# Where the second pair of heads gets its rotated keys and queries: GpSimd and DMAs in place of TensorE

## The chip, the cores and the metric

The kernel runs on one core of a Trainium2 chip. A core has TensorE (PE; its weight loads are listed as PEld), VectorE (DVE), ScalarE (ACT), GpSimd (POOL), a sync engine (SP) whose queue issues most DMAs, and 16 DMA engines. Each engine runs its own instructions in their written order and waits on semaphores. The metric is the device time in microseconds (us) of one execution, as a median of runs.

## The reference

Rotary attention over 4 batches of 8 heads (576 positions, head size 64), then a mixture of experts that chooses one of 8 experts per token. Cut to what matters:

```python
def _attn_ref(q, k, v):                       # (4, 8, 576, 64)
    def rotate(x):
        x1, x2 = (x[..., :half], x[..., half:])
        return np.concatenate([x1 * cos - x2 * sin, x1 * sin + x2 * cos], axis=-1)
    q_rot, k_rot = (rotate(q), rotate(k))
    scores = scale * np.matmul(q_rot, k_rot.transpose(0, 1, 3, 2))
    scores = scores - np.max(scores, axis=-1, keepdims=True)
    attn = np.exp(scores)
    attn = attn / (np.sum(attn, axis=-1, keepdims=True) + 1e-09)
    return np.matmul(attn, v).astype(np.float32)

def _moe_ref(x, w_gate, w_local, w1, w2):     # x: (4, 576, 512)
    ...
    # expert e of a token: argmax of x @ w_gate, or the token before's, by a local gate
    h = np.maximum(x[b, s] @ w1[e], 0.0)
    out[b, s] = p[e] * (h @ w2[e])
```

## The kernel before, in words

**Pairs and steps.** Two heads make a pair; there are 16 pairs. A pair has nine query tiles: eight of 128 queries (four for each head, tiles 0 to 7) and a tail tile (tile 8) that holds the last 64 queries of both heads. The attention loop runs over g = 0 to 143, one query tile a step; pair p has steps 9p to 9p + 8. At step g TensorE makes the scores of step g + 1 (`mm_s`, line 255, tile `s`), VectorE takes their minimum (`softmax_min`, tile `mn`; the scores carry a minus sign), ScalarE the exponential (`softmax_exp`, tile `e`, or `et` for a tail), TensorE turns the weights of step g - 2 (`tr_main`, tile `tm`), which ScalarE and VectorE split into a high and a low part (`pth`, `ptl`), and from g = 11 on TensorE multiplies with the values of the pair before (`pv_mm`, tile `pv`). The scores of one step are written s_g below, so s_9 is the first of the second pair (p = 1) and s_18 the first of the third (p = 2). After the attention come the experts, on TensorE above all.

**What a pair needs.** Float32 operands are held as a high and a low part. For tiles 0 to 7 the scores need `m_t[p]` (keys of the pair, both heads, both parts, with the high and low part of the query above each other on partitions 0 to 63 and 64 to 127) and `qst[p % 2]` (queries laid out the same way). The tail tile of pairs 2 and up needs `qtail` and `xk[p % 2]` instead.

**Two ways to make it.** The general way, for p of 2 and up: SP loads the raw queries and keys (`load_qk`, line 187, into `qkl`, a part of `stage`); GpSimd multiplies by the cosine and sine tables `tab` and adds (`rope_half`, line 199: one instruction of 1152 elements a partition, one of 576), then splits into high and low (`split_qk`, line 209, into `xq`, and `xk1` for odd pairs); twelve DMAs in SP's queue copy that into place (`spread`, line 242): two of `spread_tail`, six of `spread_k` into `m_t[p]`, four of `spread_q` into `qst`. The special way, for pairs 0 and 1, in `first_pair` (line 1111): one multiplication by the table, then TensorE adds the two halves of each head and puts them on both partition halves at once, by a matmul with a 0/1 matrix `turn` (`turned`, line 1143); ScalarE copies the high part from PSUM (line 1152 for keys, 1178 for queries) and VectorE subtracts for the low part (line 1155 for keys, 1184 for queries). For pair 1 GpSimd does the multiplications (four `products` on `raw[:, 0]`, line 1141), and the eight groups of matmuls stand in the steps 3 to 7 of the attention loop (`pair_1` in `START`, line 1246).

**What GpSimd does around there**, in its written order: two products of pair 0, the four of pair 1, `split_v(0)` (line 215), `rope_2` (both halves of pair 2, out of `raw[:, 1]`), `split_qk(2)`, `split_v(1)`, then rope and split of pair 3, and so on for each pair. **SP's queue** has, in its order: loads for pairs 0 and 1, `wid` (gate weights and the identity matrix that `tr_main` multiplies by), values, tables, raw pair 2, values, constants, `load_qk(3)`, values, `spread(2)`, `load_qk(4)`. A DMA waits in the queue until its source is there, and all behind it wait too.

**Buffers.** `m_t` and `qst` exist twice, `qtail` and `xq` once. `raw` is one of four buffers of the pool `pt`; `pth` and `ptl` of the pairs 0 and 1 take the other three and then the one of `raw`.

The lines that set the order of this:

```python
        START = {
            0: [lambda: split_v(0)], 1: [rest_q[1], lambda: keep_awake(1)], 2: [rest_q[2], lambda: load_qk(3)],
            3: [pair_1[0], pair_1[1], rope_2, lambda: split_qk(2)], 4: [pair_1[2]], 5: pair_1[3:5],
            6: pair_1[5:6], 7: pair_1[6:8] + [lambda: split_v(1), lambda: load_v(2)],
            8: [lambda: spread(2)], 40: [lambda: act.copy(trib, trif)],
        }
```

Of the kernel before, what the change touches and what calls it, by code (L numbers as in the profile page):

```python
# [24 lines left out]
P = 128  # L25
# [112 lines left out]
def tile_attention_moe(ctx, tc, qk, v, tabs, turn, consts, tri, wg, wts, out):  # L138
# [972 lines left out]
    def first_pair():  # L1111
# [34 lines left out]
        def half_keys(a, h, p=1, wait=False):  # L1146

            ps = ps_t.tile([P, 512], F32, tag="t", name=f"k{p}_{a}_{h}")
            for c, lo, n in (((0, 0, HALF),), ((0, HALF, HALF),), ((64, 0, 224), (0, 512, 64)), ((0, 224, HALF),))[2 * a + h]:
                turned(2 + a, ps[:, c:c + n], lo, n, raw[:, 0] if p else qkl)  # L1150
            hi, lo = (m_t[p][:, a, c, h * HALF:(h + 1) * HALF] for c in range(2))
# [5 lines left out]
            return rest if wait else rest()  # L1157
# [36 lines left out]
        for q in (qtail[0], *qtail0):  # L1194
            dve.memset(q.bitcast(F32), 0.0)
# [15 lines left out]
        second = [half_keys(1, h, 0, True) for h in range(2)]  # L1211
# [9 lines left out]
        return [second[2], lambda: queries(0, 256, S)(), lambda: queries(1, 256, S)()], keep_awake, pair_1  # L1221

    if True:
# [3 lines left out]
        with tc.manual_schedule():  # L1227
            rest_q, keep_awake, pair_1 = first_pair()
# [11 lines left out]
        def rope_2():  # L1240
# [7 lines left out]
            3: [pair_1[0], pair_1[1], rope_2, lambda: split_qk(2)], 4: [pair_1[2]], 5: pair_1[3:5],  # L1248
            6: pair_1[5:6], 7: pair_1[6:8] + [lambda: split_v(1), lambda: load_v(2)],
# [151 lines left out]
def _laid_out(q, k, v, moe_w_gate, moe_w_local, moe_w1, moe_w2):  # L1401
    def turned(x):
# [4 lines left out]
        for hp in range(2):  # L1407
# [5 lines left out]
    qk = np.concatenate([turned(q), turned(k)], axis=3)  # L1413
# [40 lines left out]
```

## Time and profile before

| | us |
|---|---|
| median of 3 runs | 537.85 (537.2 to 539.41) |
| the profiled execution, its own time | 537.79 |
| its span in the trace | 536.0 |
| PE busy / POOL busy / DVE busy / ACT busy, whole span | 515.5 / 346.0 / 379.1 / 344.9 |
| clock granted to TensorE, mean | 0.995 of full speed |

The span begins with the first instruction on an engine and ends with the last. The attention takes the first 290 us or so; the change is in the first 45. "Busy" of PE is modelled, so a PE that is busy all the time need not be at its peak.

### The profile page before, as it was taken

What the parts mean: (1) busy time and instruction counts of PE and PEld (TensorE: products, weight loads), DVE (VectorE), ACT (ScalarE), POOL (GpSimd) and SP (SyncE); (2) the same over time, 40 slices, a digit from 0 to 9 for tenths busy, and PEclk for the clock granted to TensorE, in tenths of its full rate; (3) what the DMA queues carried; (4) which work ended last, traced back from release to release, by engine and by line L of the source; (5) the groups of instructions that cost most, each with busy time, mean ns of one, the idle gap of its engine ahead of it and who ended that gap; (6) DMA issues with size and microseconds to landing.
All of it is one profiled execution on the core that took longest, in us unless ns stands there. A gap on an engine that the chain in (4) does not pass through costs nothing.

```text
span 536.0 us, 10810 instructions
## 1 busy us (share of the span) xinstructions
PE 515.5 (96%) x3273; PEld 459.1 (86%) x3273; DVE 379.1 (71%) x690; ACT 344.9 (64%) x766; POOL 346.0 (65%) x290
## 2 busy tenths in 40 slices
PE   7999999999999999999999899999999999999992
PEld 4889999999999999998978688887888888888881
DVE  6999999999999999999998746447421745421630
ACT  3988999999999999987866423252433344533440
POOL 4999999999999999795898202355512554411332
PEclk9999999999999999999999999999999999999998
DMA  8758878987889879866168214553637486547340
GB/s 270 285 127 224 229 211 242 239 183 213 226 225 245 206 180 238 228 162 137 24 205 230 66 32 165 169 226 105 191 101 235 141 332 181 172 102 235 98 160 25
DMA packets 65481, 97.33 MB, mean 182 GB/s; under 512 B 28353, under 2 KB 39105, under 8 KB 65282
## 3 DMA queue, kind: packets, MB, share of 16 engines
q1 hardware_dynamic: 61938, 86.45, 57.3%
q0 software_dynamic: 3040, 9.71, 5.8%
q8 instruction: 28, 0.46, 0.4%
q14 instruction: 43, 0.35, 0.2%
q10 hardware_dynamic: 432, 0.36, 0.2%
HBM read 76.95 MB, written 12.86 MB: 168 GB/s over the span
## 4 chain that ended last, share of the span: by engine, by line
PE 80%; DVE 9%; issue 3%; ACT 3%; POOL 2%; DMA 1%; ACTq 0%; POOLq 0%; SPq 0%; DVEq 0%
PE h L981 18%; PE o L1024 17%; PE pv L371 14%; PE s L273 13%; PE tm L332 9%; PE gx L457 3%; DVE mn L278 2%; PE th L1015 2%; DVE ptl L314 2%; PE tx L967 1%; ACT e L295 1%; PE tk L342 1%; DVE w L926 1%; DMA turn<-in_turn_dram 1%; DMA rows_d<-xrow 1%
## 5 line engine op out<-in xcount | busy, mean ns | idle before, releaser
L1024 PE MATMUL o<-w,hs 128*128 128x512 f32 x456 | 113.0, 398 | 0.0
L278 DVE TENSOR_REDUCE mn<-s 128x1 f32<-128x576 f32 x144 | 107.1, 745 | 2.4 <-PE s L273 1.1
L981 PE MATMUL h<-w,xs 128*128 128x512 f32 x444 | 106.1, 392 | 1.2 <-DVE xs L314 0.9
L295 ACT ACTIVATE e<-s,mn 128x576 f32<-128x576 f32 x128 | 95.4, 745 | 16.4 <-DVE mn L278 13.9
L314 DVE TENSOR_TENSOR ptl<-tm,pth 128x512 fp32r<-128x512 f32 x139 | 95.5, 688 | 11.8 <-ACT pth L310 8.8
L1030 POOL DMA_INDIRECT out_dram<-os,sidx x19 | 23.3, 1229 | 124.5 <-ACTq L932 83.0
L273 PE MATMUL s<-m,qst 128*128 128x288 f32 x512 | 96.8, 311 | 4.6 <-ACT e L295 2.7
L981 PEld LDWEIGHTS h<-w,xs 128*128 128x128 f32 x444 | 82.6, 188 | 19.4 <-DVE xs L314 1.4
L1024 PEld LDWEIGHTS o<-w,hs 128*128 128x128 f32 x456 | 83.1, 188 | 17.0 <-DVE hs L314 0.4
L310 ACT CAST pth<-tm 128x512 fp32r<-128x512 f32 x139 | 80.6, 580 | 7.1 <-PE tm L332 6.5
L273 PEld LDWEIGHTS s<-m,qst 128*128 128x128 f32 x512 | 74.1, 188 | 10.1 <-ACT e L295 5.3
L332 PE MATMUL tm<-wid,e 128*128 128x128 f32 x512 | 77.0, 272 | 0.0
L371 PE MATMUL pv<-pth,v 128*128 128x288 f32 x256 | 76.7, 315 | 0.1
L371 PE MATMUL pv<-ptl,v 128*128 128x288 f32 x256 | 76.5, 314 | 0.1
L200 POOL TENSOR_TENSOR stage<-stage 128x1152 f32<-128x1152 f32 x26 | 69.3, 2666 | 0.9 <-DMA stage<-in_qk_dram 0.9
L332 PEld LDWEIGHTS tm<-wid,e 128*128 128x128 f32 x512 | 62.1, 140 | 0.8 <-DVE ptl L314 0.4
L926 DVE TENSOR_TENSOR w<-stage,w 128x1024 fp32r<-128x1024 f32 x37 | 51.2, 1420 | 14.5 <-ACT w L923 9.7
L371 PEld LDWEIGHTS pv<-pth,v 128*128 128x128 f32 x256 | 48.3, 189 | 1.4 <-issue 0.4
L371 PEld LDWEIGHTS pv<-ptl,v 128*128 128x128 f32 x256 | 48.3, 189 | 0.5 <-POOL ptl L307 0.4
L314 DVE TENSOR_TENSOR xs<-tx,xs 128x512 fp32r<-128x512 f32 x19 | 13.1, 688 | 44.1 <-ACTq L932 34.3
L201 POOL TENSOR_TENSOR stage<-stage 128x576 f32<-128x576 f32 x26 | 37.0, 1423 | 2.0
L314 DVE TENSOR_TENSOR hs<-th,hs 128x512 fp32r<-128x512 f32 x26 | 17.5, 687 | 27.4 <-ACTq L932 15.8
(202 smaller groups left out, 822.0 us busy)
## 6 DMA issues: line engine op xcount, KB each, us to landing
stage<-in_wts_dram SPq DMA_DIRECT2D x84, 512.0 KB
stage<-in_qk_dram SPq DMA_DIRECT2D x26, 576.0 KB
qst<-xq SPq DMA_DIRECT2D x56, 128.0 KB
stage<-in_v_dram SPq DMA_DIRECT2D x16, 320.0 KB
m<-xq SPq DMA_DIRECT2D x14, 288.0 KB
m<-xk SPq DMA_DIRECT2D x14, 288.0 KB
m<-xq SPq DMA_DIRECT2D x14, 256.0 KB
m<-xk SPq DMA_DIRECT2D x14, 256.0 KB
```

The lines of the kernel that those rows point to most:

```text
L200: engine.tensor_tensor(x, x, tab[:, 2 * f:2 * f + 2], op=ALU.mult)
L201: engine.tensor_tensor(rr[:, f], x[:, 0], x[:, 1], op=ALU.add)
L273: pe.matmul(st[:, h, lo:hi], lhs, keys[:, k0:k0 + hi - lo], start=(n == 0), stop=(n == len(parts_) - 1))
L278: dve.tensor_reduce(mn, s_t[g][:, :, 0:HALF], axis=AX.XY, op=ALU.min)
L295: act.activation(dst.rearrange("p (h s) -> p h s", h=2), s_t.pop(g)[:, :, 0:HALF], AF.Exp, bias=mn, scale=-1.0, accum_out=sums[:, col:col ...
L310: act.copy(hi, src)
L314: dve.tensor_tensor(lo, src, hi.bitcast(F32), op=ALU.subtract)
L332: pe.transpose(ps[:, k], src[:, k * P:(k + 1) * P], ident)
L371: pe.matmul(pv_t[p, u], lhs.rearrange("p c d -> p (c d)"), rhs, start=(n == 0), stop=(n == 9))
L926: (pool if k in on_pool else dve).tensor_tensor(lo, src, hi.bitcast(F32), op=ALU.subtract)
L981: pe.matmul(ps[:, c], xs_t[t][:, x, k], w[y][:, c * 512:(c + 1) * 512], start=(k == 0 and n == 0), stop=(k == 3 and n == 2))
L1024: pe.matmul(ps, hs_t[t][:, x, k], w[y][:, (k % 2) * 512:(k % 2 + 1) * 512], start=(k == 0 and n == 0), stop=(k == 7 and n == 2))
```

## The change

- Pair 1 is made the general way. In `first_pair` GpSimd now multiplies its keys by their tables (two instructions), adds, splits them into `xk[1]`, ropes the queries and splits them into `xq[:, :, 0]`. The eight groups of matmuls with their copies and subtractions are gone from `START`.
- SP's queue gets the twelve spreading DMAs of pair 1, behind the load of raw pair 2. The tables for this (`tab[:, 3]` and `tab[:, 0:2]`) are loaded earlier: the first ahead of the second raw slice of pair 1, the other behind the fourth, both ahead of `wid`.
- The tail tile of pair 1 is its first step (`tile_of`), with six matmuls out of `qtail` and `xk[1]` in place of ten out of `qtail0`.
- The host lays pair 1 out like later pairs.

```diff
     def split_qk(p):
         parts = [(xq, rr)] if p % 2 == 0 else [(xk[1], rr[:, 1]), (xq[:, :, 0], rr[:, 0])]
         for x, src in parts:
-            pool.tensor_scalar(x[:, 0], src, 1.0, 1.0, op0=ALU.mult, op1=ALU.mult)
-            pool.tensor_tensor(x[:, 1], src, x[:, 0].bitcast(F32), op=ALU.subtract)
+            split_half(x, src)
+
+    def split_half(x, src):
+        pool.tensor_scalar(x[:, 0], src, 1.0, 1.0, op0=ALU.mult, op1=ALU.mult)
+        pool.tensor_tensor(x[:, 1], src, x[:, 0].bitcast(F32), op=ALU.subtract)
...
-        return p, i if p < 2 else (i + 8) % 9
+        return p, i if p < 1 else (i + 8) % 9
...
-        elif p > 1:
+        elif p > 0:
             qt, k = qtail[p % 2], xk[p % 2]
             seq = [(qt[:, x], k[:, y], whole) for x, y in PASSES]
...
-        dve.memset(raw[:, 0, :, 0:1], 0.0)
         for x in (2, 3, 0, 1):
+            if x == 3:
+                sp.dma_start(tab[:, 3], tabs[:, 3])
             sp.dma_start(raw[:, 0, x], qk[0, 1, :, x])
+        sp.dma_start(tab[:, 0:2], tabs[:, 0:2])
...
-        for x in (2, 3, 0, 1):
-            products(x, engine=pool, of=raw[:, 0])
-        m_t[1] = m_p.tile([P, 2, 2, S], F32R, tag="m", name="m_1")
-        pair_1 = [lambda a=a, h=h: half_keys(a, h) for a in range(2) for h in range(2)]
-        pair_1 += [lambda a=a, lo=lo, hi=hi: queries(a, lo, hi, 1)() for a in range(2) for lo, hi in ((0, 256), (256, S))]
...
+        for x in range(2):
+            pool.tensor_tensor(raw[:, 0, 2 + x], raw[:, 0, 2 + x], tab[:, 2 + x], op=ALU.mult)
+        pool.tensor_tensor(rr[:, 1], raw[:, 0, 2], raw[:, 0, 3], op=ALU.add)
+        split_half(xk[1], rr[:, 1])
+        rope_half(pool, 0, raw[:, 0, 0:2])
+        split_half(xq[:, :, 0], rr[:, 0])
...
         sp.dma_start(wid, wg)
         load_v(0)
-        sp.dma_start(tab[:, 3], tabs[:, 3])
         sp.dma_start(raw[:, 1], qk[0, 2])
-        sp.dma_start(tab[:, 0:2], tabs[:, 0:2])
+        spread_k(1)
+        spread_tail(1)
+        spread_q(1)
         load_v(1)
...
-            3: [pair_1[0], pair_1[1], rope_2, lambda: split_qk(2)], 4: [pair_1[2]], 5: pair_1[3:5],
-            6: pair_1[5:6], 7: pair_1[6:8] + [lambda: split_v(1), lambda: load_v(2)],
+            3: [rope_2, lambda: split_qk(2)], 7: [lambda: split_v(1), lambda: load_v(2)],
```

GpSimd's order from the products to the split of pair 2 (`stage` is the buffer of `qkl`, `tab` and `rr`; line 1141 the products, 200 and 201 a rope, 212 and 213 a split of keys or queries, 218 and 219 one of values), before:

```order
L1141 TENSOR_TENSOR stage<-stage 128x320 x2
L1141 TENSOR_TENSOR raw<-raw,stage 128x576 x4
L218 TENSOR_SCALAR v_0_228<-stage 128x10x64
L219 TENSOR_TENSOR v_0_228<-stage,v_0_228 128x10x64
L200 TENSOR_TENSOR raw<-raw,stage 128x1152
L201 TENSOR_TENSOR stage<-raw 128x576
...
L212 TENSOR_SCALAR xq<-stage 128x1152
L213 TENSOR_TENSOR xq<-stage,xq 128x1152
L218 TENSOR_SCALAR v_1_426<-stage 128x10x64
```

And the same stretch of GpSimd now (lines 1142 and 1220 are products, 1221 an addition, 215 and 216 a split of keys or queries, 221 and 222 one of values):

```order
L1142 TENSOR_TENSOR stage<-stage 128x320 x2
L1220 TENSOR_TENSOR raw<-raw,stage 128x576 x2
L1221 TENSOR_TENSOR stage<-raw 128x576
L215 TENSOR_SCALAR xk_101<-stage 128x576
L216 TENSOR_TENSOR xk_101<-stage,xk_101 128x576
L200 TENSOR_TENSOR raw<-raw,stage 128x1152
L201 TENSOR_TENSOR stage<-raw 128x576
L215 TENSOR_SCALAR xq<-stage 128x576
L216 TENSOR_TENSOR xq<-stage,xq 128x576
L221 TENSOR_SCALAR v_0_243<-stage 128x10x64
L222 TENSOR_TENSOR v_0_243<-stage,v_0_243 128x10x64
```

Two products of pair 1 went, and seven instructions came in ahead of the values of pair 0, the rope of pair 2 and its split, which follow as before.

SP's queue behind the first pair's loads, before (`m_451`, `qst_99` and the `qtail` rows are the spread of pair 2):

```order
L1201 DMA raw<-in_qk_dram 128x576 x4
L1229 DMA wid<-in_wg_dram 128x328
L197 DMA stage<-in_v_dram 128x640
L1231 DMA stage<-in_tabs_dram 128x576
L1232 DMA raw<-in_qk_dram 128x2304
L1233 DMA stage<-in_tabs_dram 128x1152
...
L193 DMA stage<-in_qk_dram 128x1152 x2
L197 DMA stage<-in_v_dram 128x640
L240 DMA qtail<-xq 64x2x64 x2
L227 DMA m_451<-xq 64x2x576
```

And now (`m_210`, `qst_100` and the first `qtail` row are the spread of pair 1):

```order
L1203 DMA raw<-in_qk_dram 128x576
L1202 DMA stage<-in_tabs_dram 128x576
L1203 DMA raw<-in_qk_dram 128x576 x3
L1204 DMA stage<-in_tabs_dram 128x1152
L1233 DMA wid<-in_wg_dram 128x328
L197 DMA stage<-in_v_dram 128x640
L1235 DMA raw<-in_qk_dram 128x2304
L230 DMA m_210<-xk_101 64x1152
...
L243 DMA qtail<-xq 64x2x64 x2
L238 DMA qst_100<-xq 64x512 x4
L197 DMA stage<-in_v_dram 128x640
```

The tables moved ahead of `wid`, and the spread of pair 1 stands between the load of raw pair 2 and the next values.

TensorE at the change from pair 1 to pair 2, before (`s_659` is s_17, the tail of pair 1 with ten matmuls; `s_691` is s_18, the tail of pair 2; `s_714` is s_19):

```order
L273 MATMUL s_659<-m_201,qtail_136 128x288 x6
L273 MATMUL s_659<-m_201,qtail_136 128x224
...
L273 MATMUL s_691<-xq,qtail 128x288 x6
L332 MATMUL tm_702<-wid,e_3_639 128x128 x4
L273 MATMUL s_714<-m_451,qst_99 128x288 x4
```

And now (`s_645` is s_17, `s_672` s_18, `s_694` s_19):

```order
L276 MATMUL s_645<-m_210,qst_100 128x288 x4
...
L276 MATMUL s_672<-xq,qtail 128x288 x6
L335 MATMUL tm_682<-wid,e_2_591 128x128 x4
L276 MATMUL s_694<-m_431,qst_99 128x288 x4
L335 MATMUL tm_703<-wid,e_3_650 128x128 x4
```

s_17 lost its ten matmuls of a tail, and between s_18 and s_19 there is as little as before: the four turning matmuls of one step.

## Rows read from the trace of the kernel before

**Rows 1.** The page's slices: busy tenths in 40 slices of 13.4 us.

```profile
PE   7999999999999999999999899999999999999992
POOL 4999999999999999795898202355512554411332
```

**Rows 2.** Chain that ended last, first 60 us: start us, us, what.

```profile
18.22 0.81 DVE m L1155 x2
...
27.50 0.15 DVE qtail L1184
...
30.90 0.80 PE s L273 x4
...
39.85 1.16 PE s L273 x10
...
45.62 0.53 PE s L273 x4
```

**Rows 3.** Timeline of GpSimd: start us, us, engine, line, op, out<-in, [idle before <-releaser].

```profile
9.20 1.43 POOL L1141 TENSOR_TENSOR raw<-raw,stage 128x576 f32<-128x576 f32 x1
11.10 4.14 POOL L1141 TENSOR_TENSOR raw<-raw,stage 128x576 f32<-128x576 f32 x3 [0.47 <-DMA raw<-in_qk_dram]
15.20 0.73 POOL L218 TENSOR_SCALAR v<-stage 128x640 fp32r<-128x640 f32 x1
...
27.08 2.68 POOL L213 TENSOR_TENSOR xq<-stage,xq 128x1152 fp32r<-128x1152 f32 x1
29.71 0.74 POOL L218 TENSOR_SCALAR v<-stage 128x640 fp32r<-128x640 f32 x1
...
36.17 2.68 POOL L200 TENSOR_TENSOR stage<-stage 128x1152 f32<-128x1152 f32 x1
38.93 1.43 POOL L201 TENSOR_TENSOR stage<-stage 128x576 f32<-128x576 f32 x1
40.33 0.67 POOL L212 TENSOR_SCALAR xk<-stage 128x576 fp32r<-128x576 f32 x1
...
42.49 0.67 POOL L212 TENSOR_SCALAR xq<-stage 128x576 fp32r<-128x576 f32 x1
...
44.64 2.67 POOL L200 TENSOR_TENSOR stage<-stage 128x1152 f32<-128x1152 f32 x1
```

**Rows 4.** Timeline of SP's queue: start us, us that issuing took, DMAs.

```profile
29.78 1.37 SPq L240 DMA_DIRECT2D qtail<-xq  x2
31.26 0.59 SPq L227 DMA_DIRECT2D m<-xq  x1
...
36.37 3.01 SPq L235 DMA_DIRECT2D qst<-xq  x4
39.47 1.25 SPq L193 DMA_DIRECT2D stage<-in_qk_dram  x2
```

**Rows 5.** Half-microsecond windows: length, engines' busy us (instructions), granted clock, DMA share, GB/s.

```profile
11.00:11.50 0.50, 0.02 (x1) 0.00 (x0) 0.47 (x2) 0.18 (x1) 0.40 (x1) 1.00 0.95 273
11.50:12.00 0.50, 0.00 (x0) 0.00 (x0) 0.47 (x2) 0.50 (x2) 0.50 (x1) 1.00 0.97 354
...
41.00:41.50 0.50, 0.50 (x7) 0.50 (x6) 0.49 (x2) 0.18 (x2) 0.42 (x1) 1.00 0.40 119
41.50:42.00 0.50, 0.50 (x6) 0.50 (x6) 0.30 (x1) 0.47 (x1) 0.50 (x1) 1.00 0.94 373
```

**Rows 6.** Timeline of TensorE: s_9, s_10, s_19, s_20 and, in pair 3, s_28.

```profile
25.39 0.93 PE L273 MATMUL s<-m,qst 128*128 128x288 f32 x4
...
27.31 0.78 PE L273 MATMUL s<-m,qst 128*128 128x288 f32 x4 [0.54 <-DVE qst L1184]
...
43.50 0.80 PE L273 MATMUL s<-m,qst 128*128 128x288 f32 x4
...
45.46 0.69 PE L273 MATMUL s<-m,qst 128*128 128x288 f32 x4
...
59.96 0.79 PE L273 MATMUL s<-m,qst 128*128 128x288 f32 x4
```

**Rows 7.** Windows at the end of pair 3's spread and at the span's end.

```profile
55.50:56.00 0.50, 0.50 (x6) 0.50 (x5) 0.47 (x2) 0.50 (x2) 0.50 (x1) 1.00 0.62 111
...
526.00:528.00 2.00, 0.13 (x1) 0.00 (x0) 0.00 (x0) 0.69 (x1) 0.88 (x1) 1.00 0.02 4
528.00:530.00 2.00, 0.00 (x0) 0.00 (x0) 0.00 (x0) 0.00 (x0) 0.10 (x1) 1.00 0.18 60
530.00:536.00 6.00, 0.00 (x0) 0.00 (x0) 0.00 (x0) 0.00 (x0) 0.00 (x0) 0.58 0.00 0
```

**Rows 8.** Timeline of TensorE before its first real matmul: the ten waking ones.

```profile
1.19 4.33 PE L1136 MATMUL wake_ps<-wake 128*128 128x512 bf16 x10 [1.19 <-DVE one_c L1188]
```

More of the change, by code (lines that the diff above doesn't have):

```diff
@@ L268, in mm_s @@
         else:
-            seq = [(qtail0[p][:, a], m[:, a, c], (whole, turned)[a]) for a in range(2) for c in range(2)]
+            seq = [(qtail0[:, a], m[:, a, c], (whole, turned)[a]) for a in range(2) for c in range(2)]
         for h in range(2):
@@ L1126, in first_pair @@
         m_t[0] = m_p.tile([P, 2, 2, S], F32R, tag="m", name="m_0")
-        qtail0 = et_p.tile([P, S], F32R, tag="et", name="qtail0")[:, 0:4 * P].rearrange("p (n a s) -> p n a s", n=2, a=2)
-        qtail0 = [qtail0[:, n] for n in range(2)]
+        qtail0 = et_p.tile([P, S], F32R, tag="et", name="qtail0")[:, 0:2 * P].rearrange("p (a s) -> p a s", a=2)
         dve.memset(wake, 0.0)
@@ L1144, in turned, with half_keys @@
             pe.matmul(dst, sel, of[:, x, lo:lo + n], start=True, stop=True)
[L1146 to L1151, printed above, removed]
+        def half_keys(h):
+            ps = ps_t.tile([P, 512], F32, tag="t", name=f"k_1_{h}")
+            for c, lo, n in (((64, 0, 224), (0, 512, 64)), ((0, 224, HALF),))[h]:
+                turned(3, ps[:, c:c + n], lo, n)
+            hi, lo = (m_t[0][:, 1, c, h * HALF:(h + 1) * HALF] for c in range(2))
             act.copy(hi, ps[:, 0:HALF])
@@ L1155, in rest @@
                 dve.tensor_tensor(lo, ps[:, 0:HALF], hi.bitcast(F32), op=ALU.subtract)
-            return rest if wait else rest()
+            return rest
         def keys(a):
@@ L1169, in keys, with queries @@
             return rest
-        def queries(a, lo, hi, p=0):
-            ps = ps_t.tile([P, 512], F32, tag="t", name=f"q{p}_{a}_{lo}")
-            turned(a, ps[:, 0:hi - lo], lo, hi - lo, raw[:, 0] if p else qkl)
+        def queries(a, lo, hi):
+            ps = ps_t.tile([P, 512], F32, tag="t", name=f"q_{a}_{lo}")
+            turned(a, ps[:, 0:hi - lo], lo, hi - lo)
             parts = []
@@ L1176, in queries @@
                 if c1 > c0:
-                    dst, src = qtail0[p][:, a, 64 * a:64 * a + 64] if c0 == 512 else qst[p][:, a, c0:c1], ps[:, c0 - lo:c1 - lo]
+                    dst, src = qtail0[:, a, 64 * a:64 * a + 64] if c0 == 512 else qst[0][:, a, c0:c1], ps[:, c0 - lo:c1 - lo]
                     act.activation(dst, src, AF.Copy, scale=-0.125)
@@ L1193, in first_pair @@
         dve.memset(onesb, 1.0)
-        for q in (qtail[0], *qtail0):
+        for q in (qtail[0], qtail0):
             dve.memset(q.bitcast(F32), 0.0)
@@ L1210, in first_pair @@
         queries(0, 0, 256)()
-        second = [half_keys(1, h, 0, True) for h in range(2)]
+        second = [half_keys(h) for h in range(2)]
         second.append(queries(1, 0, 256))
@@ L1215, in first_pair @@
             f()
-        for x in (2, 3, 0, 1):
-            products(x, engine=pool, of=raw[:, 0])
-        m_t[1] = m_p.tile([P, 2, 2, S], F32R, tag="m", name="m_1")
-        pair_1 = [lambda a=a, h=h: half_keys(a, h) for a in range(2) for h in range(2)]
-        pair_1 += [lambda a=a, lo=lo, hi=hi: queries(a, lo, hi, 1)() for a in range(2) for lo, hi in ((0, 256), (256, S))]
-        return [second[2], lambda: queries(0, 256, S)(), lambda: queries(1, 256, S)()], keep_awake, pair_1
+        for x in range(2):
[4 more added lines that the diff above has]
+        split_half(xq[:, :, 0], rr[:, 0])
+        return [second[2], lambda: queries(0, 256, S)(), lambda: queries(1, 256, S)()], keep_awake
     if True:
@@ L1227, in tile_attention_moe @@
         with tc.manual_schedule():
-            rest_q, keep_awake, pair_1 = first_pair()
+            rest_q, keep_awake = first_pair()
         sp.dma_start(wid, wg)
         load_v(0)
-        sp.dma_start(tab[:, 3], tabs[:, 3])
         sp.dma_start(raw[:, 1], qk[0, 2])
-        sp.dma_start(tab[:, 0:2], tabs[:, 0:2])
+        spread_k(1)
+        spread_tail(1)
+        spread_q(1)
         load_v(1)
@@ L1401, in _laid_out, with turned @@
 def _laid_out(q, k, v, moe_w_gate, moe_w_local, moe_w1, moe_w2):
-    def turned(x):
+    def turned(x, own):
         t = x.reshape(B, NP, 2, S, 2, D // 2).transpose(0, 1, 2, 4, 5, 3)
@@ L1405, in turned @@
         x[:, :, 1] = x[:, :, 1, :, ::-1].copy()
-        for hp in range(2):
+        for hp in range(own):
             y = x[0, hp].copy()
@@ L1411, in turned @@
         return x.reshape(B, NP, P, 2, S)
-    qk = np.concatenate([turned(q), turned(k)], axis=3)
+    qk = np.concatenate([turned(q, 1), turned(k, 1)], axis=3)
     vp = v.reshape(B, NP, 2, S, D)
```

## The prediction

> **What bounds the kernel now.** I first read the page's slices [rows 1]: TensorE is busy in nearly all of the span, and GpSimd is just as full from the second slice to the sixteenth, so two engines run without reserve through the attention. The chain that ended last [rows 2] then says which of them sets the end. From 18 to 28 us it runs through VectorE, and nine of its pieces there, the first and the last of them shown, are the low parts of pair 1's keys and queries; together they hold 3.6 us. From 30.9 us on its pieces are TensorE's, one behind the other: the scores of a step, the turned weights, the values. So there the steps go at TensorE's pace, and whatever holds TensorE up once after about 31 us is not won back.
>
> Next, whether GpSimd is early or late, since no wait on it shows. Its timeline [rows 3] has it start on pair 1 at 9.20, wait 0.47 us for a raw slice at 11.10, and then work without a gap: values of pair 0 at 15.20, pair 2 split at 29.71, pair 3 at 44.64. SP's queue [rows 4] issues the first spreading DMA of pair 2 at 29.78, at the moment GpSimd has done, and the last behind 36.37 + 3.01 = 39.38. The share of the DMA engines [rows 5] falls to 0.40 between 41.0 and 41.5 and rises again with the 373 GB/s of the next load: the last packets of the spread moved at about 41.2. And s_19, the first step that needs it, starts at 43.50 [rows 6]. Pair 2 is there 2 to 3 us before it is wanted. That is the reserve that the change draws on.
>
> **The change part by part.** *Removed from VectorE, ScalarE and TensorE:* the eight groups of pair 1. On the chain that is the 3.6 us of VectorE [rows 2]; ScalarE's copies and TensorE's turning lie beside it. The tail of pair 1 leaves s_17, where its ten matmuls held 1.16 us of chain against 0.53 of an ordinary tile: 0.6 us less [rows 2]. These 4.2 us are what can be won, if pair 1 and pair 2 are there in time.
>
> *GpSimd's order.* Removed: products of pair 1, 1.43 + 4.14 us [rows 3]. Added, from rows of the same shape: two products, an addition of 1.40 (38.93 to 40.33), a split of keys of 2.16 (40.33 to 42.49), a rope of the queries of 4.16 (36.17 to 40.33), a split of 2.15 (42.49 to 44.64) [rows 3]. The second product waits for its raw slice, and now `tab[:, 3]` with 288 KB is ahead of that. Before, the slice was there at 11.10; the queue moved 273 and then 354 GB/s [rows 5], so 288 KB more take until about 12.0. From there: 12.0 + 1.38 (a third of 4.14) + 1.40 + 2.16 + 4.16 + 2.15 = 23.25, against 15.20 before. Everything behind on GpSimd comes **8.05 us later**. The bounds: 7.15 if the slice comes no later than before, 8.95 if it comes twice as late as that.
>
> *Pair 1's own data.* The keys are split at 16.9 and their six DMAs take SP until about 22. The queries are split at 23.25; two DMAs for the tail (1.37 us of issuing) and the four of `qst` (3.01) follow [rows 4]. As the last packets of pair 2 moved 1.8 us after the last issue (41.2 less 39.38), s_9 gets its tail at about 26 and s_10 its queries at about 28.4, against starts of 25.39 and 27.31 before [rows 6]. So pair 1 is about 1.1 us late, not early: the 3.6 us are free on VectorE and can't be used. With the 0.6 us of s_17 given back, TensorE would come to s_19 at about 44.0.
>
> *Pair 2's data.* GpSimd has split pair 2 at 29.71 + 8.05 = 37.76 [rows 3]. SP is idle by then and issues as before, so the spread ends at 41.2 + 8.05 = 49.2. s_19 needs the third DMA of the four to `qst`, 0.75 us ahead of the last (3.01 / 4); with 0.2 us for its landing, 48.7. TensorE's order has nothing to put between: behind s_18 stand four turning matmuls and then s_19. So s_19 starts at **48.7 in place of 43.50: 5.2 us later**. The bounds: s_19 did not wait for a DMA before, so the reserve is at least nothing and, by the packets, at most 43.50 less 40.45, about 3.0; the delay lies between 7.15 - 3.0 = 4.1 and 8.95 us.
>
> *What goes with it at no cost.* `wid` lands later, behind 864 KB of tables, and `tr_main` waits for it at 14 us; some 2 us at the rates of [rows 5]. What hides that is the wait of s_9 for its tail; without it pair 0 would lose them. `ptl` of pair 1 takes the buffer of `raw`, which rope_2 now reads until 23.25 + 2.3 + 8.3 = 33.9; VectorE first writes it at step 11, at about the same time, and up to 0.3 us there is covered by the wait at s_19. The values of pair 0 come at 25.6, before step 11.
>
> *After s_19.* TensorE's pieces follow each other as before [rows 2], so nothing is won back. Does GpSimd hold it up once more? It is 8.05 us late and TensorE 5.2, so each later pair has 2.85 us less reserve. Pair 3's spread ends in the slice 55.5 to 56.0 and s_28 starts at 59.96 [rows 6, 7]: a reserve of about 4, which stays above nothing.
>
> *A rule of the skill against a row.* The spread of pair 2 is 1,728 KB and moves from 31.3 to 41.2, at some 180 GB/s. The Trainium skill, "DMA: Bandwidth & Descriptors", section "Why small descriptors are slow (HBM only)", says that transfers from SBUF to SBUF are not slowed by small descriptors and run against the fabric's limit. By that rule the spread would be faster than this and leave a larger reserve. This trace differs, and the measurement decides; what the rule would make of the time is the fourth rival.
>
> **Sum.** 537.79 of the profiled execution + 5.2 = 543.0 us. The median of the three runs is 537.85, 0.06 above that execution.
>
> **The rivals.**
> 1. *TensorE's clock falls.* After s_18 TensorE has nothing from about 43.9 to 48.7. At the end of the span it had its last matmul at 526.1, the granted clock was 1.00 until 530 and 0.58 in the mean of 530 to 536 [rows 7]: idle, it fell to the low level (1.2 GHz), after about as long a rest as this one. At the start the ten waking matmuls of 512 columns took 4.33 us [rows 8], 0.43 us each, which is 1.2 GHz. If the clock falls just before s_19 and the next 4.3 us run at half speed, 2.15 us more are lost: 545.1. Against it: the longest rest of TensorE in the attention before was 1.2 us, and no row shows a fall there. The Trainium skill, "TensorE: Matmul & The Clock Gate", section "Why this matters for your kernels", warns that idle time between bursts of matmuls halves the clock.
> 2. *TensorE ends up at GpSimd's pace.* If pair 3 or 4 is late too, all 8.05 us appear: 545.8. It decides once the reserve of pair 3 (about 4) is under 2.85. Against it: [rows 7].
> 3. *Not slower: the reserve covers it.* Place: the spread of pair 2 ahead of s_19. If pair 2 is late by no more than the 2 to 3 us of reserve, s_19 keeps its own pace, 44.0 against 43.50: 538.3. The point from which it decides is a shift of GpSimd of 2.8 us, and I find 7.15 at the least, from instructions that all have rows; I would have to be wrong on what s_19 waits for.
> 4. *The spread moves at the rate of a load.* At the 373 GB/s of [rows 5] its 1,728 KB take 4.7 us in place of 9.9; pair 2 would be there at 44.0 and nothing lost at s_19: 538.3 again. This is the rule of the skill above, and the traces bear it out nowhere; SP's issuing alone [rows 4] takes 8 us of those 9.9.
> 5. *Faster.* If pair 1 were also there in time, the 4.2 us would come through: 533.6. It needs GpSimd to be done with pair 1 before 20 us.
>
> **How the numbers follow.** The forecast 0.50, rival 1 0.22, rival 2 0.08, rival 3 0.13, rival 4 0.02, rival 5 0.05. The likeliest is the forecast: 543.0. Its own bounds are 541.9 to 546.7; the range takes in rivals 1 and 2 at the upper end and reaches down towards rival 3 to 540.0, which leaves out the 0.20 of the rivals 3 to 5: 540.0 to 546.7. A measurement of this kernel can tell about 0.5% from no change, 2.7 us. Faster by more than that: 0.05 (rival 5). Within: 0.15 (rivals 3 and 4). Slower: 0.80.
>
> **What would show it right or wrong.** GpSimd's split of pair 2 should end near 37.8, the first `qtail` DMA of pair 2 follow at once, and TensorE wait for a DMA ahead of s_9 and, for 4 to 5 us, ahead of s_19, which starts near 48.7. VectorE should have gaps from 15 to 28 us, with 4 us less to do, and GpSimd 7 us more. Steps behind s_19 should stand 5.2 us later all the way, at an equal pace. If s_19 starts before 46, the reserve was larger than I read. If the granted clock is below 1.00 behind s_19, rival 1 holds. If the lag grows again at s_28 or s_37, rival 2 does.

## The result, and the profile after

The changed kernel takes 545.11 us (median of 4 runs, 543.46 to 545.56) against 537.53 (4 runs) for the kernel before: 1.0138 times as long, 95% interval 1.0119 to 1.0158. The profiled execution took 545.18, its span is 543.3. The forecast was 543.0, its range 540.0 to 546.7.

The slices on the page of the changed kernel ("after" from here on; "before" is the kernel before), 13.6 us each, answer to [rows 1]; PEclk is the granted clock in tenths:

```profile
PE   7797999999999999999998899999999999999992
POOL 4999999999999999896698302337511455411331
PEclk9978999999999999999999999999999999999996
```

TensorE and GpSimd are as full as before, but TensorE has a dip in the second and the fourth slice, and its clock one in the third and the fourth. GpSimd's timeline in after answers to [rows 3] (start, us, engine, line, op, out<-in, idle before):

```profile
9.86 2.89 POOL L1220 TENSOR_TENSOR raw<-raw,stage 128x576 f32<-128x576 f32 x2 [0.58 <-DMA raw<-in_qk_dram]
12.83 1.42 POOL L1221 TENSOR_TENSOR stage<-raw 128x576 f32<-128x576 f32 x1
...
21.46 1.44 POOL L216 TENSOR_TENSOR xq<-stage,xq 128x576 fp32r<-128x576 f32 x1
22.86 0.73 POOL L221 TENSOR_SCALAR v<-stage 128x640 fp32r<-128x640 f32 x1
...
37.36 0.73 POOL L221 TENSOR_SCALAR v<-stage 128x640 fp32r<-128x640 f32 x1
```

The values of pair 0 follow at 22.86 in place of 15.20, those of pair 1 (and with them the end of pair 2's split) at 37.36 in place of 29.71: 7.65 us later. SP's queue answers to [rows 4]:

```profile
37.42 1.29 SPq L243 DMA_DIRECT2D qtail<-xq  x2
...
43.89 3.78 SPq L238 DMA_DIRECT2D qst<-xq  x4
47.76 1.03 SPq L193 DMA_DIRECT2D stage<-in_qk_dram  x2
```

And TensorE answers to [rows 6]: s_9, s_10, s_18, s_19.

```profile
25.62 1.23 PE L276 MATMUL s<-xk,qtail 128*128 128x288 f32 x6 [1.86 <-DMA qtail<-xq]
28.25 1.30 PE L276 MATMUL s<-m,qst 128*128 128x288 f32 x4 [0.55 <-DMA qst<-xq]
...
43.62 0.96 PE L276 MATMUL s<-xq,qtail 128*128 128x288 f32 x6
49.07 0.77 PE L276 MATMUL s<-m,qst 128*128 128x288 f32 x4 [4.05 <-DMA qst<-xq]
```

s_19 waits 4.05 us for pair 2's queries and starts at 49.07 in place of 43.50. The 2-us windows (length, busy us of PE, PEld, DVE, ACT, POOL with counts, granted clock, DMA share, GB/s) show the clock behind each of the two rests:

```profile
24.00:26.00 2.00, 0.38 (x3) 0.41 (x4) 0.75 (x2) 1.11 (x3) 2.00 (x2) 1.00 0.42 92
...
28.00:30.00 2.00, 1.75 (x8) 1.77 (x9) 1.10 (x2) 1.05 (x3) 2.00 (x2) 0.50 0.94 311
...
50.00:52.00 2.00, 2.00 (x12) 2.00 (x10) 1.33 (x2) 1.51 (x4) 1.92 (x3) 0.54 1.01 401
52.00:54.00 2.00, 2.00 (x12) 1.98 (x12) 0.83 (x2) 0.69 (x2) 2.00 (x2) 0.60 0.76 286
```

To see where the time goes I compare, step by step, the start of VectorE's minimum (`mn`) with that of the same step before. The "lag" below is that difference. In after it is -1.9 us at step 8, +2.4 at 13, +1.9 at 18, **+5.2 at 19, +6.5 at 21**, and it then stays at 6.3 to 6.5 until step 143; the last matmul is 6.6 later and the end of the span 7.3. Read alone this says: 5.2 at s_19 as forecast, 1.2 of low clock behind it (rival 1), and no further place at which GpSimd's lateness costs anything. The experiments show that the last part of this is not so: there is a second such place, which this run just misses.

### The profile page after: what moved, and what is told of

It reads as the page before. It is cut to its first block, busy times and chain, and to the rows that moved or that the text cites. A ratio compares the mean times of both kernels' runs of the same rounds, so it can differ in the third digit from the quotient of the medians.

```text
span 543.3 us, 10765 instructions
## 1 busy us (share of the span) xinstructions
PE 515.6 (95%) x3251; PEld 459.4 (85%) x3251; DVE 375.0 (69%) x678; ACT 342.1 (63%) x756; POOL 352.8 (65%) x295
## 5 line engine op out<-in xcount | busy, mean ns | idle before, releaser
L276 PE MATMUL s<-m,qst 128*128 128x288 f32 x512 | 97.9, 314 | 8.6 <-DMA qst<-xq 4.6
L276 PEld LDWEIGHTS s<-m,qst 128*128 128x128 f32 x512 | 75.5, 192 | 14.1 <-ACT e L298 5.6
L335 PE MATMUL tm<-wid,e 128*128 128x128 f32 x512 | 78.3, 276 | 0.4 <-DMA wid<-in_wg_dram 0.4
L335 PEld LDWEIGHTS tm<-wid,e 128*128 128x128 f32 x512 | 63.2, 142 | 1.4 <-DMA wid<-in_wg_dram 0.6
```

Of the source, the lines that this page charges most:

```text
L335: pe.transpose(ps[:, k], src[:, k * P:(k + 1) * P], ident)
```

## The experiments

Every run has a lag at step 23 (behind s_19), at 37 and at 40. "GpSimd" is how much later than before (29.71) the split of pair 2 ends there; "rest" is TensorE's wait for a DMA ahead of s_19. The lags are those of the one profiled execution, the medians those of all runs. The ratio compares with runs of the kernel before from the same session, whose median was 537.5 to 538.0.

| kernel | median us | ratio to before (95%) | GpSimd | rest | lag 23 | lag 37 | lag 40 |
|---|---|---|---|---|---|---|---|
| after | 545.11 | 1.0138 (1.0119 to 1.0158) | 7.65 | 4.05 | 6.47 | 6.46 | 6.46 |
| late1 | 539.39 | 1.0033 (1.0014 to 1.0052) | 2.69 | 0.95 | 0.64 | 0.62 | 1.59 |
| late3 | 544.90 | 1.0139 (1.0109 to 1.0170) | 8.01 | 5.15 | 7.11 | 7.09 | 7.12 |
| no_rope2 | 540.05 | 1.0046 (1.0023 to 1.0069) | 1.65 | none | 0.70 | 0.70 | 1.32 |
| awake | 544.96 | 1.0128 (1.0107 to 1.0148) | 8.23 | filled | 5.58 | 5.57 | 6.48 |
| keys_first | 546.58 | 1.0151 (1.0127 to 1.0175) | 8.46 | none | 1.93 | 3.69 | 7.37 |
| after_st | 554.89 | 1.0317 (1.0270 to 1.0364) | 8.19 | 4.52 | 7.05 | 7.08 | 7.07 |
| awake_st | 555.98 | 1.0353 (1.0310 to 1.0396) | 8.19 | filled | 4.96 | 4.98 | 4.98 |
| kf_st | 556.29 | 1.0350 (1.0314 to 1.0387) | 8.00 | none | 2.85 | 3.16 | 3.74 |
| awake_h | 545.05 | 1.0140 (1.0111 to 1.0169) | 8.53 | filled | 5.42 | 5.42 | 6.62 |
| kf_h | 544.64 | 1.0136 (1.0100 to 1.0171) | 8.01 | none | 1.48 | 3.24 | 6.13 |
| best | 545.63 | 1.0141 (1.0116 to 1.0166) | 5.6 | none | 6.99 | 7.00 | 7.04 |

**1 and 2. GpSimd made late, and nothing else.** The kernel before, with extra products ahead of pair 2's rope (late3 is shown; late1 has `idle_pool(1)`):

```diff
+        def idle_pool(n):
+            for _ in range(n):
+                pool.tensor_tensor(rr[:, 0:2], raw[:, 1, 2:4], tab[:, 2:4], op=ALU.mult)
-            3: [pair_1[0], pair_1[1], rope_2, lambda: split_qk(2)], ...
+            3: [pair_1[0], pair_1[1], lambda: idle_pool(3), rope_2, lambda: split_qk(2)], ...
```

> The kernel before with one more product of 1152 elements on GpSimd (about 2.66 us) ahead of the rope of pair 2; its result is overwritten and nobody reads it. Pair 1 stays on TensorE, SP's queue is as before. Theory (GpSimd's lateness in excess of a reserve of 2 to 3 us at s_19 is the loss): the split of pair 2 ends at 32.4, its spread at 43.9, s_19 starts between 43.5 and 43.9 in place of 43.50, and the time is within 0.5 us of before, 537.5 to 538.2. Rival (there is no reserve, each us of GpSimd counts): s_19 at 46.2, +2.7 us. Rival (the loss comes from pair 1's own spread or from SP's queue, GpSimd's order is innocent): no change here and none with three products.

> The same with three such products, about 8.0 us, which is what the change adds to GpSimd ahead of pair 2 (7.65 us measured). Nothing else of the change is in. Theory: the split of pair 2 ends at 37.7, s_19 starts at about 48.7 to 49.1, TensorE rests for some 5 us ahead of it, its clock falls behind it as in the changed kernel (1.2 us more), and the time is 5.2 to 6.6 us above before: 543 to 544.5. Rival (no reserve): the same plus 2.5. Rival (the cause is pair 1's spread in SP's queue, or pair 1 being late): no change.

With three products, GpSimd and TensorE of late3:

```profile
17.30 8.11 POOL L1242 TENSOR_TENSOR stage<-raw,stage 128x1152 f32<-128x1152 f32 x3
...
37.72 0.72 POOL L218 TENSOR_SCALAR v<-stage 128x640 fp32r<-128x640 f32 x1
```

```profile
42.40 1.03 PE L273 MATMUL s<-xq,qtail 128*128 128x288 f32 x6
49.02 1.30 PE L273 MATMUL s<-m,qst 128*128 128x288 f32 x4 [5.15 <-DMA qst<-xq]
```

That is the changed kernel's loss without its change: s_19 at 49.02, a clock at 0.50 from 45.7, in the rest, to 52.5, and 544.90 us, 0.4 above the range that I had given. Pair 1's spread in SP's queue is not needed for it. With one product, 2.69 us of lateness become 0.6 us at s_19, so the reserve there is about 2.1 (2.69 less 0.64), inside the 2 to 3 of the forecast. But I expected no more than 0.5 us in all, and 1.5 were measured (539.39 against 537.94): a further 1.0 us comes at step 38. VectorE there, in late1:

```profile
80.96 0.42 DVE L471 TENSOR_TENSOR xrow<-gx,sum 128x256 f32<-128x256 f32 x1 [1.10 <-DMA rows_d<-xrow]
```

**3. The clock.** Seven matmuls that nobody reads, in the rest ahead of s_19 of the changed kernel:

```diff
+                if g == 18:
+                    fill = ps_t.tile([P, 512], F32, tag="t", name="fill")
+                    for _ in range(7):
+                        pe.matmul(fill[:, 0:328], ident, wid.rearrange("p a n -> p (a n)"), start=True, stop=True)
                 if g + 1 < NSTEP:
                     mm_s(g + 1)
```

> The changed kernel with seven more matmuls (128 by 328, float32, some 0.55 us each, into a PSUM tile that nobody reads) between s_18 and s_19, in TensorE's rest of 4.05 us. Theory (behind s_19 the clock is low for 3.4 us because TensorE rested, and this costs 1.2 us): s_19 starts at about 49.1 as before, the clock stays at 1.00 from 50 to 54, steps 21 and later stand 1.2 us earlier than in the changed kernel, 544.0. Rival (the lag that grows behind s_19 is GpSimd's pace or late values, the clock only goes with it): no change, 545.1. If the seven hold TensorE past the landing of the queries, s_19 itself comes later by as much.

TensorE, and the window that showed 0.54 in after:

```profile
45.38 4.03 PE L1289 MATMUL fill<-wid 128*128 128x328 f32 x14
49.62 0.77 PE L276 MATMUL s<-m,qst 128*128 128x288 f32 x4 [0.22 <-PE fill L1289]
```

```profile
50.00:52.00 2.00, 2.00 (x18) 2.00 (x18) 1.27 (x2) 1.13 (x3) 1.92 (x3) 1.00 0.89 325
```

The clock stays up, and the lag no longer grows behind s_19: 5.78 at step 19, 5.58 at 23. Locally the theory holds. The time is the same (544.96 against 545.11), as the rival had it, but for another reason: at step 38 the lag goes from 5.57 to 6.48, in the same place as in late1, where VectorE waits 1.04 us for a DMA out of `xrow`:

```profile
85.85 0.42 DVE L474 TENSOR_TENSOR xrow<-gx,sum 128x256 f32<-128x256 f32 x1 [1.04 <-DMA rows_d<-xrow]
```

I had missed a second place at which TensorE pays for GpSimd's lateness.

**4. Pair 2's keys first.** GpSimd ropes and splits keys, then queries, and the keys' DMAs go out beside the work on the queries:

```diff
         def rope_2():
             for f in (1, 0):
                 rope_half(pool, f, raw[:, 1, 2 * f:2 * f + 2])
+                split_half(xq[:, :, f], rr[:, f])
+
+        def spread_2():
+            spread_k(2)
+            spread_tail(2)
+            spread_q(2)
...
-            3: [rope_2, lambda: split_qk(2)], ...
+            3: [rope_2], ...
-            8: [lambda: spread(2)], ...
+            8: [spread_2], ...
```

> The changed kernel, but pair 2 is made in two halves on GpSimd, keys first: rope and split of the keys, then rope and split of the queries, and its spread in the order keys, tail, queries. GpSimd does the same work and ends at the same time. Theory (s_19 waits because all twelve spreading DMAs of pair 2, some 10 us of issuing and moving, stand behind the last GpSimd instruction at 37.4): the six DMAs of the keys now go out from about 33 on, beside the work on the queries, and only the tail and the queries follow it, so s_19 finds its queries at about 43 to 44.5 and starts at 45 to 46, held by the pace of pair 1 and not by a DMA; the clock doesn't fall behind it; 539.5 to 541. Rival (SP's queue, or the moving of 1.7 MB, is the limit whatever the order): s_19 after 47.5, over 543.

s_19 starts at 45.82, 3.2 us earlier, and waits for no DMA. The kernel is not faster but slower, 546.58. The lag is 1.93 at step 23, 3.55 at step 28, 7.63 at step 38. At step 28 I take the wait to be for the spread of pair 3, whose last DMA into `m` is issued at 61.46, 2.2 us before s_28 starts; the profile names ScalarE's `et`, which is not what s_28 needs: in the kernel before, s_28 started at 59.96 and `et` at 60.67. No run tests this. TensorE at s_19, and VectorE at step 38:

```profile
45.82 0.80 PE L276 MATMUL s<-m,qst 128*128 128x288 f32 x4 [0.16 <-ACT e L298]
```

```profile
82.72 0.18 DVE L473 TENSOR_TENSOR gm<-gx,sum 128x36 f32<-128x36 f32 x1
86.75 0.42 DVE L474 TENSOR_TENSOR xrow<-gx,sum 128x256 f32<-128x256 f32 x1 [3.84 <-DMA rows_d<-xrow]
```

Behind this wait TensorE's clock is low once more, from 89.5 to 92.9, and the lag goes on from 7.4 at step 40 to 8.5 at step 45.

What these rows are: with every pair GpSimd and VectorE each write a tile `xrow`, stored to `rows_d` by three DMAs in SP's queue. VectorE's tile waits until the store of an earlier one has left its buffer. Those stores stand in the queue behind a spread and behind the next load of raw keys and queries, and both wait for GpSimd. The store that matters was issued at 71.04 before, and VectorE took the buffer at 79.13 without waiting:

```profile
71.04 0.54 SPq L481 DMA_DIRECT2D rows_d<-xrow  x1
```

```profile
79.13 0.41 DVE L471 TENSOR_TENSOR xrow<-gx,sum 128x256 f32<-128x256 f32 x1
```

In after it is issued at 79.13, and VectorE takes the buffer at 85.58, again without waiting:

```profile
76.40 1.55 SPq L193 DMA_DIRECT2D stage<-in_qk_dram  x2
78.04 0.38 SPq L484 DMA_DIRECT2D rows_d<-xrow  x1
78.48 0.56 SPq L488 DMA_DIRECT2D rows_d<-xrow  x1
79.13 0.54 SPq L484 DMA_DIRECT2D rows_d<-xrow  x1
```

```profile
85.58 0.41 DVE L474 TENSOR_TENSOR xrow<-gx,sum 128x256 f32<-128x256 f32 x1
```

Four of the kernels kept this order and waited; in them VectorE went on 5.8 to 7.2 us after that issue (awake 80.07 to 85.85, keys_first 80.63 to 86.75, late1 74.81 to 80.96, no_rope2 73.53 to 80.69). For after that gives 84.9 to 86.3, and VectorE came to it at 85.58: it seems that the s_19 wait and the clock had just made TensorE late enough not to meet it. late3, with a lag of 7.1, came at 86.23, 6.1 us after the issue, and waited for nothing either.

**5 to 8. The stores ahead of the load.** To take this wait away I moved the load behind the stores, in after, with the filler, and with keys first:

```diff
-                    if p + 3 < NPAIR:
-                        load_qk(p + 3)
+                if i == LOAD_AT and 1 <= p and p + 3 < NPAIR:
+                    load_qk(p + 3)
```

`LOAD_AT` is 2: the load goes into the queue two steps later. The fourth of these kernels, both_st, also moves the splits of pair 1 off GpSimd.

> The changed kernel with one order turned round in SP's queue from pair 4 on: the three stores of attention rows (to rows_d, 288 KB) ahead of the load of the next raw keys and queries (1.15 MB), which waits for GpSimd, and not behind it. This takes a wait away that the run with matmuls in the rest showed: at step 38 VectorE's write of xrow waited 1.0 us for such a store, 3.8 us with the keys first. Theory (two floors lie close together in the changed kernel: 5.2 us at s_19 with 1.2 us of low clock behind it, and some 6 us at step 38): without the second floor the first still stands, steps 21 to 45 at +6.3 to +6.6, 545.0. Rival (the loss is GpSimd's pace through the stores alone): 543.5 or less.

> The same turned order with the seven matmuls in TensorE's rest ahead of s_19. Theory (clock and stores are alternatives, so that either alone changes nothing): clock 1.00 behind s_19, +5.5 us from step 21 on and still +5.5 at step 45, 544.0, about 1 us less than with either alone. Rival (the step at 38 has nothing to do with the stores): +6.5 at step 45 again, 544.9.

> Keys of pair 2 first, with the same turned order. Without it s_19 was only 2.3 us late, but s_28 brought the lag to 3.6 and step 38, where VectorE waited 3.8 us for a store, to 7.6. Theory (GpSimd stays 8 us late for the whole attention, and each thing that waits for it presents that again, less its own reserve: 2.3 us at s_19, 5 at s_28, about 1 at the stores): with the stores ahead of the load the step at 38 is gone, steps 40 to 72 at +3.5 to +4, 541 to 542. Rival (VectorE or TensorE is short of time by itself after step 36): still +8 at step 45, over 545.

> Keys of pair 2 first, the turned order, and the two splits of pair 1 on ScalarE and VectorE in place of GpSimd (which saves GpSimd 4.3 us). Theory (all lags follow from GpSimd's 7.7 us): GpSimd is only some 4 us late, its rope of pair 2 starts near 21; s_9 and s_10 come some 2 us earlier than in the changed kernel, s_19 waits for nothing, no floor at s_28 and at step 38; the time is 0 to 2 us above before, 537.5 to 540, 5 us or more below the changed kernel. Rival (the splits on ScalarE and VectorE, which stand in order with the exponentials, hold the steps of pair 0 up by more than they bring): s_9 no earlier than 25.6, over 541.

The wait at step 38 is gone or nearly gone where it was the question: awake_st goes through it at 4.98 (VectorE below), where awake had 6.48; in kf_st VectorE still waits 0.75 us there, in place of 3.84, and the lag is 3.74 at step 40, where keys_first had 7.37. after_st, which keeps the wait at s_19 and the low clock, stays at 7.05 to 7.08 from step 23 to 40. So s_19 with its clock, and the stores, are two places at which TensorE pays for the same lateness of GpSimd, and taking one away leaves the other.

```profile
84.01 0.18 DVE L473 TENSOR_TENSOR gm<-gx,sum 128x36 f32<-128x36 f32 x1
84.11 0.42 DVE L474 TENSOR_TENSOR xrow<-gx,sum 128x256 f32<-128x256 f32 x1
```

In total the first three are 10 to 11 us worse than after, which I had not foreseen. The load now waits for stores, and GpSimd for the load (awake_st below, GpSimd). In after_st GpSimd waits so seven times, 10.8 us in all; it comes 8.2 us late to the values of pair 1 and 18.3 us late to those of pair 12. TensorE shows that late: its lag is still 7.0 at step 100, jumps at steps 109 and 127 to 129, and is 17.5 at step 132 (18.4 in awake_st). Where the edit was to remove one wait it made a new one on the engine without reserve.

```profile
86.12 2.66 POOL L200 TENSOR_TENSOR stage<-stage 128x1152 f32<-128x1152 f32 x1 [2.08 <-DMA stage<-in_qk_dram]
```

both_st (562.89 us) says nothing on the theory: its split of pair 1's queries stands behind pair 2's rope, so that it splits pair 2's queries in their place, and ScalarE and VectorE wait for it, VectorE 12.7 us.

**9 and 10. The stores between the halves of the load**, keys' half first:

```diff
                     if p + 3 < NPAIR:
-                        load_qk(p + 3)
+                        load_half(p + 3, 1)
+                if i == 2 and 1 <= p and p + 3 < NPAIR:
+                    load_half(p + 3, 0)
```

> The changed kernel with seven matmuls in TensorE's rest, and with the three stores of attention rows placed in SP's queue between the two halves of the next load (keys, stores, queries), not ahead of all of it. The whole load behind the stores took the wait of step 38 away, but GpSimd then waited 2.6 us for its raw keys at 86 us and the lag grew from step 60 on. Theory: the clock stays at 1.00 behind s_19, steps 21 to 54 stand +5.0 to +5.6 after before, VectorE doesn't wait at step 38, GpSimd doesn't wait for raw keys, and the lag stays that to the end: 543.0 to 544.0. Rival (any store ahead of a part of the load costs GpSimd more than it gives): over 546.

> Keys of pair 2 first, with the stores between the halves of the load. Theory (with s_19 and the stores out of the way, what is left is GpSimd's lag less the reserve at s_28 and later): +3 to +4 at steps 28 to 72, and to the end if nothing else is short, 541 to 542. Rival: GpSimd, 8 us late and without a gap, presents its lag at another place: over 544.

Neither theory held; the rival of kf_h (over 544) did, with 544.64. GpSimd no longer falls further behind with every pair (8.5 us late at pair 1's values and 8.6 at pair 11's in awake_h), but step 38 costs again: awake_h goes from 5.42 to 6.62, kf_h from 3.24 to 6.13. With half a load ahead the stores are still too late. The mechanism is the same, the remedy too weak.

**11. GpSimd relieved.** Four splits (pair 1's keys and queries, the values of pairs 0 and 1) move to ScalarE (high part) and VectorE (low part), with keys first and the stores between the halves. With the splits, the spread of pair 1 and the loads behind it in SP's queue move too, `load_qk(3)` among them:

```diff
+        def split_1(x, src):
+            act.copy(x[:, 0], src)
+            dve.tensor_tensor(x[:, 1], src, x[:, 0].bitcast(F32), op=ALU.subtract)
...
+            3: [keys_1], 6: [lambda: split_v(0, True)], 5: [queries_1, rope_2], 8: [spread_2], 9: [lambda: split_v(1, True), lambda: load_v(2)],
```

> The kernel with the keys of pair 2 first and the stores between the halves, and GpSimd relieved: the splits of pair 1's keys and queries and of the values of the pairs 0 and 1 (8.9 us of GpSimd) are made by ScalarE and VectorE in steps 3, 5, 6 and 9. Theory (all the lags are GpSimd's 7.7 us seen at different places): GpSimd is no later than before, pair 1 is split some 3 us earlier than in the changed kernel, s_9 starts at 23.5 to 24.5 without a rest behind which the clock falls, s_10 at 25.5 to 26.5, s_19, s_28 and step 38 wait for nothing; 535.5 to 538, equal to before or up to 2 us under it, 7 or more under the changed kernel. Rival (the splits on ScalarE and VectorE hold the steps of pair 0 up by as much): s_10 after 27.3, 538 to 540.

545.63 us, ratio 1.0141 (1.0116 to 1.0166): no gain, and above both ranges given. s_9 starts at 29.81, 4.2 us later than in after. The reason begins in VectorE's rows and in GpSimd's of the same stretch:

```profile
18.58 3.00 DVE L1242 TENSOR_TENSOR xk<-stage,xk 128x576 fp32r<-128x576 f32 x1
...
24.56 1.47 DVE L1242 TENSOR_TENSOR xq<-stage,xq 128x576 fp32r<-128x576 f32 x1
```

```profile
18.33 2.64 POOL L200 TENSOR_TENSOR raw<-raw,stage 128x1152 f32<-128x1152 f32 x1
21.73 1.40 POOL L201 TENSOR_TENSOR stage<-raw 128x576 f32<-128x576 f32 x1 [0.76 <-DVE xk L1242]
...
23.98 1.44 POOL L216 TENSOR_TENSOR xq<-stage,xq 128x576 fp32r<-128x576 f32 x1
```

GpSimd's product ends at 20.97 (18.33 + 2.64) and VectorE's subtraction at 21.58, 0.61 after it; the second one ends at 26.03, again 0.61 after the GpSimd instruction beside it (23.98 + 1.44): VectorE had been standing behind GpSimd. In both_st a subtraction of the same shape ran with GpSimd at rest and took 0.76 us:

```profile
34.99 0.76 DVE L1237 TENSOR_TENSOR xq<-stage,xq 128x576 fp32r<-128x576 f32 x1 [12.66 <-ACT xq L1236]
```

The steps of pair 0 waited meanwhile, TensorE rested 2.86 us at 20.3, and its clock was low from 22.4 to 39.5. The six DMAs of pair 1's keys go out only behind that subtraction, from 21.61 on (16.55 in after), the tail's behind them at 26.55, and s_9 waits for the tail:

```profile
23.17 1.33 PE L281 MATMUL s<-m,qst 128*128 128x288 f32 x4 [2.86 <-ACT e L303]
...
29.81 1.54 PE L281 MATMUL s<-xk,qtail 128*128 128x288 f32 x5 [1.16 <-DMA qtail<-xq]
```

GpSimd was not relieved either: `load_qk(3)` is issued at 33.86 (28.81 in after), and pair 3's rope starts 9.2 us later than before, 7.6 in after. So this run doesn't test its theory.

**12. GpSimd's lateness taken away, the rest of the change kept.** After without pair 2's rope; what is split is the buffer's old content, pair 1's rotated values:

```diff
-            3: [rope_2, lambda: split_qk(2)], ...
+            3: [lambda: split_qk(2)], ...
```

> The changed kernel without the rope of pair 2: GpSimd splits what stands in the buffer in its place, so that pair 2's scores are computed from pair 1's rotated values. That takes 8.15 us out of GpSimd's order and nothing else; pair 1 goes by GpSimd and the spreading DMAs as in the change. GpSimd will wait some 3 us for the DMAs that read xq before it writes pair 2 there, so pair 2 is split near 32 in place of 37.4. Theory (the loss is GpSimd's lateness, seen at s_19 and again at step 38): s_9 at 25.6 and s_10 at 28.3 as in the changed kernel, s_19 at 45 to 45.5 without a wait for a DMA, no rest, no low clock behind it, no wait at step 38; what is left is pair 1's own lateness with the low clock behind s_9, +1.5 to +2.4 from step 20 to the end, 539.5 to 540.5. Rival (the twelve DMAs of pair 1 in SP's queue, or pair 1 being late, carry the loss): still over 543.

The median is 540.05, inside the range that I had given (the runs spread from 538.20 to 543.85, the profiled one took 538.95). TensorE at s_9, s_10 and s_19:

```profile
25.71 1.03 PE L276 MATMUL s<-xk,qtail 128*128 128x288 f32 x6 [1.87 <-DMA qtail<-xq]
28.32 1.30 PE L276 MATMUL s<-m,qst 128*128 128x288 f32 x4 [1.15 <-DMA qst<-xq]
...
44.60 0.80 PE L276 MATMUL s<-m,qst 128*128 128x288 f32 x4 [0.15 <-ACT e L298]
```

Pair 1 is as late as in after, s_19 waits for no DMA, and the lag is 0.70 behind it, less than the 1.5 to 2.4 that I expected; the clock behind s_9 was low for 3.4 us here and for 6.8 in after. At step 38 VectorE waits 0.78 us for the store even here, which I had not expected; the lag is 1.3 from there on. So of after's 6.5 us of lag some 5 to 6 go with GpSimd's lateness (6.46 less 1.32, or less 0.70). What is left is pair 1's own lateness and what the 1.65 us by which GpSimd is still late cost at step 38; no run parts the two.

## Why the prediction was right, point by point

**GpSimd's order**: 8.05 us forecast, 7.65 measured. The second raw slice landed at about 11.4, not 12.0 (its product ends at 12.75); the other terms came to 10.11 us in place of 9.87. (The chain of [rows 2] has eight pieces of pair 1 on VectorE, not nine; their sum of 3.6 us is right.)

**Pair 1's data**: s_9 was expected at about 26 and s_10 at 28.4; they came at 25.62 and 28.25. The wait for `wid` was 0.41 us, not 2. VectorE's busy time is 4.1 us less and GpSimd's 6.8 more, against 4 and 7.

**s_19**: 48.7 forecast, 49.07 measured; GpSimd was 0.4 earlier than I said, and the four `qst` issues took 3.78 in place of 3.01, so that the agreement to 0.4 us is in part luck. The reserve of 2 to 3 us is confirmed by late1 (2.1). late3 and no_rope2 show, from both sides, that the wait was caused by what I said. Rival 4 fell: pair 2's spread took from 37.42 to about 49, as long as before.

**What was mis-sized**: "the longest rest" as evidence against rival 1. The clock did fall behind s_19, and also behind s_9 after only 1.86 us without a matmul, from 26.3 to 33.1; the lag grows from -0.8 to +2.4 between steps 9 and 13. The later wait at s_19 hides that. Behind s_19 it is 1.2 us by the lag, not the 2.15 of the rival. TensorE came to s_19 at 45.0 (49.07 less 4.05) and not at 44.0. By the sign that the prediction set (a clock below 1.00 behind s_19) rival 1 holds, and its 545.1 is what was measured. That it fits to 0.1 us is luck: the clock cost about half of what the rival says, and 0.4 at s_19 and 0.9 at the end, which it doesn't name, make up the rest.

**The step that failed**: "Does GpSimd hold it up once more?", which I answered from pair 3's spread alone. That reserve is indeed large: with GpSimd 8.5 us late in keys_first the lag at s_28 was 3.55, so some 5 us, against the 4 I read. But `xrow` and its stores depend on GpSimd's pace as well, through SP's queue, and their reserve before was only 0.9 to 2.3 us (71.04 + 5.8 to 7.2, against 79.13). Rival 2 was thus right in its mechanism and wrong in its place, and I gave it 0.08. It did not show in after, as it seems because rival 1 had cost about as much already. The forecast missed 2.2 us of 545.18. By TensorE's own starts these are 0.4 at s_19 (5.57 us late in place of 5.2), 0.9 up to step 23 (6.46 us late; the clock, in whose place the stores cost as much in awake), and 0.9 behind that: the last matmul is 6.63 later and the end of the span 7.29, where the kernels differ by up to a microsecond either way (late1's end is 1.27 later with a last matmul 2.22 later). VectorE's minimum of step 19 is only 5.2 late, so the lag gives the clock 1.2.

**Left open**: none of these kernels beat the one before. One more buffer for `xrow` should remove the second wait without touching SP's order; on-chip memory, as the kernel lays it out, has no room for it, and no run tests it. What the low clock behind s_9 costs by itself was not measured either.

## What to carry to other kernels

An engine without gaps that is given more work stays late: in after GpSimd took back only the 0.9 us that it had waited for a load at 60 us before, and of its 7.65 us 6.6 were left at the values of pair 3 and of pair 12 alike. Each place that waits for this engine costs the lateness less its own reserve; in these runs the total was the largest of these, with what the clock added behind the wait, and not the first or their sum. Before costing such a move, list all who wait for the engine, also through a queue or a buffer that comes free late, and read the reserve of each; removing the first wait alone may bring nothing, as keys_first showed, and moving a queue's order to remove the second may cost more than both, as the kernels with the stores ahead showed. An experiment that adds lateness and nothing else (late1, late3) finds these places for the price of one line.

## What the runs showed of the hardware

A VectorE subtraction with both operands in on-chip memory (SBUF; 128x576, float32) took 0.76 us with GpSimd at rest (both_st) and 3.00 us when GpSimd's 2.64 us product had started just ahead of it (best). The Trainium skill, "SBUF — State Buffer", section "Who interferes with whom", says that the two engines share a pair of ports which one holds for its whole instruction; this trace agrees, with VectorE ending 0.61 us behind GpSimd, twice. After rests of 1.86 (after), 2.86 (best), 4.05 (after) and 5.15 us (late3) TensorE's granted clock was seen at 0.50, its lower level of 1.2 GHz, for 6.8, 17.1, 3.4 and 6.8 us, in best and late3 from within the rest on: the length of the rest does not order the length of what follows. With seven unused matmuls in the rest ahead of s_19 (awake) it stayed at 1.00. The Trainium skill, "TensorE: Matmul & The Clock Gate", section "Why this matters for your kernels", warns of idle gaps between bursts of matmuls; this trace agrees, and shows it behind a gap as short as 1.86 us.
